# Attention and a soft mixture of experts on one core: the last term of a sum added in PSUM, a division moved behind the second layer, and loads of 2 MB in place of 1 MB

## The chip, the core and the metric

The kernel runs on one core of a Trainium2 chip. The metric is device time in microseconds (us) of one execution, as the median over runs. The core has TensorE (PE, matrix products), VectorE (DVE), ScalarE (ACT), GpSimd (POOL), and SyncE (SP), whose queue issues nearly all transfers; 16 DMA engines carry them between the main memory (HBM) and the on-chip memory (SBUF). TensorE writes its results to PSUM, from where VectorE or ScalarE copies them out. All data is 32-bit floating point.

## The reference

For 8 batches of 8 heads, with x of 512 tokens and state of 32 rows, each of width 64:

```python
# attention, per batch and head
a  = softmax(x @ state.T / 8);  xread = a  @ state     # 512 x 64
a2 = softmax(state @ x.T / 8);  sread = a2 @ x         # 32 x 64
X  = concat([xread, sread])     # all heads: 8 * 544 = 4352 tokens of width 512
# soft mixture of experts, 8 experts of 4 slots each
logits = X @ phi                                  # 4352 x 32
d = exp(logits - logits.max(0)); d /= d.sum(0) + 1e-9
slot_input = (d.T @ X).reshape(8, 4, 512)
for e in range(8):
    slot_out[e] = maximum(slot_input[e] @ w1[e], 0) @ w2[e]     # 512 -> 1024 -> 512
c = softmax(logits, axis=1)
out = c @ slot_out
```

w1 and w2 have 16.8 MB each, x 8.4 MB, the output 8.9 MB.

## The kernel before

There are three stages. The first goes through the 8 batches. A batch of x (1 MB) is turned by TensorE (`X`), scored against the state (`S`), brought to rows by VectorE's 32x32 transposes (`q`), and both softmaxes run over VectorE, GpSimd and ScalarE; `R` computes sread and is the last reader of the batch's x. Logits are computed from the attention weights without forming xread (`Lx`, with G = state times phi in `G_sb`).

The sum d.T @ X is kept as a running sum. `y` is a 128x128 tile that holds the sum so far, relative to a running maximum; each new group of two batches (0 to 3) has its exponentials `dx`, a product `T` into the PSUM tile tp, a transpose `tt`, a product `Px` with the state, and `Y`, which multiplies y by the rescaling factor `al` and adds the new term on VectorE. `Ls` to `Ys` do the same for the state's tokens. `l_row` is the running sum of the exponentials. The last steps are `Wd` (sum of l over the partitions, a product), `We` (add 1e-9 and take the reciprocal, on VectorE), `Yf` (the identity times 1/l, on ScalarE), `Y.3`, `SI` (y turned and divided in one product with that tile) and `SIe`, four copies on VectorE into two tiles si_m, from which layer 1 takes its weights. Two products `W` on a constant tile stand between them.

The order of all these steps is a list written out by hand, `ORDER`; each engine does its part in the order in which the steps are called.

The second stage is layer 1 (`w1_part`, two halves of 512 columns, 8 experts each) and the first half of layer 2's columns (`wide_part`). The third computes the rest of layer 2 in pieces (`more`) between the outputs. `so_sum` sums partial results with a product and copies them to so_r on ScalarE; `out` multiplies so_r by the softmax c, copies 2 times 2 tiles to SBUF on ScalarE and VectorE, and issues a store of 1 MB.

Loads come through pools of buffers: `big` has 13 buffers of 1 MB and `pairs` 4 of 2 MB. x takes 8 of the big ones. `todo` lists the weights in the order of loading; `load_w(n)` issues the next n, and is called at the start (13), after each batch's `R`, and inside layer 1. Issuing a load into a used buffer waits, on SP's queue, for that buffer's last readers, and for the transfer eight places before it. Five pieces of w2 go to places that other data leave (`load_part`). The last four loads (layer 3 in `todo`) are 2 MB each already.

Of the kernel before, what the change touches and what calls it, by code (L numbers as in the profile page):

```python
# [24 lines left out]
NBIG = 13  # L25
NPAIR = 4
# [27 lines left out]
Lus.1 A.7.0 lkp.1 A.6.0 dx.3 D.1 dT.3 ad.7.1 Px.2 ad.6.0 ae.7.0 dTe.3 Ps.1 al.3 Y.2 Ys.1 Lu.3 T.3 tt.3 Wd We Px.3  # L54
W.256 Yf Y.3 SI W.128 SIe
# [8 lines left out]
def attention_soft_moe(ctx: ExitStack, tc: tile.TileContext, x0, x1, x, st0, st1, w1, w2a, w2b, out_x, out_s):  # L64
# [37 lines left out]
    todo = [(1, hf, e) for hf in range(2) for e in range(E)]  # L102
    todo += [(2, k, e) for k in range(2) for e in range(0, E, 2)]
    last = todo.pop()
    todo += [(3, 0, 0), (3, 0, 4), last, (3, 1, 0), (3, 1, 4)]
    both = []

    def load_w(n):
        for _ in range(min(n, len(todo))):
            layer, k, e = todo.pop(0)  # L110
            if layer == 3:
                t = pairs.tile([P, 4 * F], F32, tag="pair", name=f"w3_{k}_{e}")
# [4 lines left out]
                continue  # L117
            if layer == 1 and len(w1t) < 8 * NPAIR:
                if not both:
                    t = pairs.tile([P, 4 * F], F32, tag="pair", name=f"w1_{k}_{e}")  # L120
                    both.extend((t[:, 0 : 2 * F], t[:, 2 * F :]))
                t = both.pop(0)
            else:
                t = big.tile([P, 2 * F], F32, tag="big", name=f"w{layer}_{k}_{e}")
            if layer == 1:
                t = t.rearrange("p (k f) -> p k f", k=4)
                nc.sync.dma_start(t, w1[k, e])
                for i in range(4):
                    w1t[k, e, i] = t[:, i]
            else:  # L130
                t = t.rearrange("p (e k f) -> p e k f", e=2, k=4)
                nc.sync.dma_start(t, w2a[e // 2, k])
                for i in range(8):
                    w2t[layer, k, e + i // 4, i % 4] = t[:, i // 4, i % 4]
# [39 lines left out]
    with ExitStack() as actx:  # L174
# [162 lines left out]
        def R_(b, h):  # L337
# [12 lines left out]
            if h == 1:  # L350
# [280 lines left out]
        def We():  # L631
            Z["rl"] = sm.tile([P, 1], F32, tag="rl", name="rl", bufs=1)
# [23 lines left out]

        def windows():
            for k in range(2):
# [3 lines left out]
        def SIe():  # L662
            for k in range(4):
                dve.tensor_copy(slots(si_m[k // 2], k % 2), Z["p"][:, k, :].rearrange("p (e c) -> p e c", c=4))
# [13 lines left out]
        (k1, e1), (k2, e2) = [todo.pop(B)[1:] for _ in range(2)]  # L678
# [16 lines left out]
        def w1_part(hf, e):  # L695
# [85 lines left out]
        def so_sum(k, half_of=0):  # L781
# [6 lines left out]
            act.copy(so_r[i // 2][:, P * (i % 2) : P * (i % 2) + P], p)  # L788

        def out(k, q):  # L790
# [12 lines left out]
            ot = big.tile([P, NJ, 512], F32, tag="big", name=f"out{k}_{q}")  # L803
# [146 lines left out]
```

## Time and profile before

| | |
|---|---|
| time, median of 3 runs | 129.68 us (129.62 to 129.85) |
| the profiled execution | 129.54 us, span 127.8 us |
| TensorE busy | 116.7 us (91%), granted clock 0.974 of full on the mean |
| VectorE, ScalarE, GpSimd busy | 86.7, 76.9, 44.8 us |
| bytes moved by DMA | 51.74 MB, mean 405 GB/s |
| layer 1 starts | 76.01 us |
| first output issued, last output issued | 102.17 us, 121.24 us |

The span runs from the first to the last instruction; the rest of an execution's time lies around it. Busy shares are over the whole span, and a kernel like this one has stages with different limits: to judge a change, the stretch in which it acts has to be read. A load that is issued early lands late without any harm, as long as the queue in front of it is full; what counts is the rate at which the queue is worked off.

### The profile page before, as it was taken

What the parts mean: (1) busy time and instruction counts of PE and PEld (TensorE: products, weight loads), DVE (VectorE), ACT (ScalarE), POOL (GpSimd) and SP (SyncE); (2) the same over time, 40 slices, a digit from 0 to 9 for tenths busy, and PEclk for the clock granted to TensorE, in tenths of its full rate; (3) what the DMA queues carried; (4) which work ended last, traced back from release to release, by engine and by line L of the source; (5) the groups of instructions that cost most, each with busy time, mean ns of one, the idle gap of its engine ahead of it and who ended that gap; (6) DMA issues with size and microseconds to landing.
All of it is one profiled execution on the core that took longest, in us unless ns stands there. A gap on an engine that the chain in (4) does not pass through costs nothing.

```text
span 127.8 us, 4698 instructions
## 1 busy us (share of the span) xinstructions
PE 116.7 (91%) x1992; PEld 80.5 (63%) x1992; DVE 86.7 (68%) x194; ACT 76.9 (60%) x189; POOL 44.8 (35%) x63
## 2 busy tenths in 40 slices
PE   5989999999999999999999999999999999998600
PEld 2737686789686869858767869952465655575200
DVE  2348999999999999999986759019930355442700
ACT  4039999999999999999965711310100445635700
POOL 3005266391947467557882105803500000000000
PEclk9999999999999999999999999999999999999955
DMA  4999999999999999999999999999999999999993
GB/s 130 345 410 423 423 426 423 428 423 421 423 423 426 416 436 416 421 431 418 426 418 433 416 421 398 448 423 441 413 441 415 436 383 412 421 419 420 386 430 139
DMA packets 8229, 51.74 MB, mean 405 GB/s; under 512 B 912, under 2 KB 1040, under 8 KB 3216
## 3 DMA queue, kind: packets, MB, share of 16 engines
q1 hardware_dynamic: 7920, 50.92, 95.9%
q10 hardware_dynamic: 288, 0.52, 1.1%
q8 instruction: 15, 0.25, 0.7%
q14 instruction: 6, 0.05, 0.1%
HBM read 42.53 MB, written 8.91 MB: 403 GB/s over the span
## 4 chain that ended last, share of the span: by engine, by line
PE 72%; DVE 10%; DMA 6%; ACT 3%; issue 2%; SPq 1%; POOL 0%; DVEq 0%; ACTq 0%; POOLq 0%
PE so_ps L760 12%; PE h_ps L697 11%; PE xt_ps L226 8%; PE o L796 7%; DMA st_phi<-st_in 6%; PE sc L245 5%; PE sr_ps L343 4%; PE an_ps L309 4%; PE eT_ps L309 4%; PE lt L378 3%; PE t_ps L503 2%; DVE sums L274 2%; DVE q L258 2%; DVE aT L290 1%; DVE m L263 1%
## 5 line engine op out<-in xcount | busy, mean ns | idle before, releaser
L267 POOL TENSOR_TENSOR q<-q,m 128x512 f32<-128x512 f32 x16 | 16.8, 1051 | 15.7 <-DVE m L263 5.2
L231 ACT ACTIVATE xt<-xt_ps 128x512 f32<-128x512 f32 x30 | 18.0, 618 | 5.7 <-PE xt_ps L226 5.5
L226 PE MATMUL xt_ps<-ident,x 128*128 128x128 f32 x128 | 18.4, 282 | 0.5 <-DMA x<-x_in 0.5
L285 POOL TENSOR_TENSOR q<-q,rr 128x512 f32<-128x512 f32 x16 | 16.6, 1051 | 5.1 <-DVE rr L280 3.6
L226 PEld LDWEIGHTS xt_ps<-ident,x 128*128 128x128 f32 x128 | 14.6, 144 | 3.8 <-PE sc L245 1.4
L760 PE MATMUL so_ps<-w,h_m 128*32 128x128 f32 (+1 forms) x376 | 15.5, 309 | 0.0
L807 DVE COPY out<-o 128x512 f32<-128x512 f32 x14 | 9.2, 687 | 9.0 <-PE o L796 8.8
L760 PEld LDWEIGHTS so_ps<-w,h_m 128*32 128x32 f32 x376 | 10.4, 110 | 7.2 <-issue 4.6
L697 PE MATMUL h_ps<-w,si_m 128*32 128x512 f32 x128 | 14.4, 594 | 0.1
L296 DVE TENSOR_REDUCE nm<-sc 128x1 f32<-128x512 f32 x16 | 10.6, 670 | 2.2 <-PE sc L245 2.2
L806 ACT COPY out<-o 128x512 f32<-128x512 f32 x14 | 7.7, 588 | 6.8 <-PE o L796 6.7
L697 PEld LDWEIGHTS h_ps<-w,si_m 128*32 128x32 f32 x128 | 9.1, 110 | 3.9 <-issue 2.9
L301 ACT ACTIVATE e<-sc,nm 128x512 f32<-128x512 f32 x16 | 11.3, 709 | 0.4 <-DVE nm L296 0.2
L258 DVE STREAM_TRANSPOSE q<-sc 128x512 f32<-128x512 f32 x16 | 11.1, 695 | 0.1
L290 DVE STREAM_TRANSPOSE aT<-q 128x512 f32<-128x512 f32 x16 | 10.9, 689 | 0.3 <-POOL q L285 0.2
L343 PE MATMUL sr_ps<-x,eT 128*32 128x64 f32 x512 | 10.5, 221 | 0.1
L274 DVE TENSOR_REDUCE sums<-q 128x16 f32<-128x512 f32 x16 | 10.4, 663 | 0.2 <-ACT q L270 0.2
L263 DVE TENSOR_REDUCE m<-q 128x16 f32<-128x512 f32 x16 | 10.4, 658 | 0.0
L270 ACT ACTIVATE q<-q 128x512 f32<-128x512 f32 x16 | 10.4, 650 | 0.0
L309 PE MATMUL eT_ps<-ident,e 128*128 128x128 f32 x64 | 9.8, 279 | 0.0
L245 PE MATMUL sc<-xt,st_phi 64*32 64x512 f32 x128 | 9.6, 601 | 0.0
L343 PEld LDWEIGHTS sr_ps<-x,eT 128*32 128x32 f32 x512 | 8.7, 110 | 1.5 <-issue 1.0
(126 smaller groups left out, 186.2 us busy)
## 6 DMA issues: line engine op xcount, KB each, us to landing
w<-w_in SPq DMA_DIRECT2D x16, 1024.0 KB, 19.7
w<-w2b_in SPq DMA_DIRECT2D x4, 2048.0 KB, 15.0
x<-x_in SPq DMA_DIRECT2D x7, 1024.0 KB, 13.9
w<-w2a_in SPq DMA_DIRECT2D x6, 1024.0 KB, 19.5
out_x<-out SPq DMA_DIRECT2D x6, 1024.0 KB, 5.8
out_x<-out SPq DMA_DIRECT2D x4, 512.0 KB, 4.7
w<-w2a_in SPq DMA_DIRECT2D x4, 256.0 KB, 14.5
x<-x_in ACTq DMA_DIRECT2D x2, 256.0 KB, 3.9
```

The lines of the kernel that those rows point to most:

```text
L226: pe.transpose(p[:, P * j : P * j + P], xb[b][:, g, j, :], ident)
L231: act.mul(r[f"xt{g}"], r[f"xp{g}"], 0.125)
L245: pe.matmul(r[f"sp{h}"][32 * g : 32 * g + 32, :], st_t(b, g)[64 * h : 64 * h + 64, :], r[f"xt{g}"][64 * h : 64 * h + 64, :], start=True, s ...
L258: dve.transpose(r[f"q{h}"], r[f"sp{h}"])
L267: pool.tensor_tensor(v, v, R[b][f"m1{h}"].broadcast_to([P, 16, NS]), op=ALU.subtract)
L274: dve.tensor_reduce(out=v, in_=R[b][f"qv{h}"], axis=AX.X, op=ALU.add)
L285: pool.tensor_tensor(v, v, r.broadcast_to([P, 16, NS]), op=ALU.mult)
L290: dve.transpose(r[f"aT{h}"], r[f"q{h}"])
L309: pe.transpose(p[:, j, :], r[f"{src}{h}"][:, P * j : P * j + P], ident)
L343: pe.matmul(r["srp"][32 * g : 32 * g + 32, h, :], r[f"eT{h}"][:, j, 32 * g : 32 * g + 32], xb[b][:, g, j, D * h : D * h + D], start=(j == ...
L697: pe.matmul(h_ps[hf][32 * kt : 32 * kt + 32, :], si_m[kt // 2][:, 256 * (kt % 2) + 32 * e : 256 * (kt % 2) + 32 * e + 32], w1t[hf, e, kt], ...
L760: pe.matmul(so[k][32 * i : 32 * i + 32, :], h_m[hf][:, 256 * i + 32 * e : 256 * i + 32 * e + 32], w(i), start=(hf == 0 and e == 0), stop=( ...
```

## The change

Loads: `big` has 3 buffers and `pairs` 9, all of x lies in pairs, and x4 with x5, x6 with x7, six pairs of experts of w1, and two quarters of w2 (`w2c`, a new input array made of the same numbers) come in one transfer of 2 MB each. Two pairs of w1 still come in two transfers. The order of the weights changes: three loads of w2 now stand before the last three pairs of w1. `load_w` is called after four batches instead of all. Outputs take halves of pairs. No byte is added.

The sum: `Px.3` and `Y.3` are gone. `SIa` turns y and multiplies it by the last factor al (the identity times al, `Yf`), leaving the sum open in PSUM; `ttz` transposes tp in two halves of 64 rows into a cleared tile tz (the place of `G_sb`, cleared by GpSimd in `windows`); `SIb` adds the state times tz into the same PSUM tiles. The copies `SIe` alternate between VectorE and ScalarE. 1/l is no longer part of it; `so_sum` multiplies by it, which is the same since maximum(., 0) passes a positive factor. The two `W` products are gone.

```diff
-NBIG = 13
-NPAIR = 4
+NBIG = 3
+NPAIR = 9
...
-Lus.1 A.7.0 lkp.1 A.6.0 dx.3 D.1 dT.3 ad.7.1 Px.2 ad.6.0 ae.7.0 dTe.3 Ps.1 al.3 Y.2 Ys.1 Lu.3 T.3 tt.3 Wd We Px.3
-W.256 Yf Y.3 SI W.128 SIe
+Lus.1 A.7.0 lkp.1 A.6.0 dx.3 D.1 dT.3 ad.7.1 Px.2 ad.6.0 ae.7.0 dTe.3 Ps.1 al.3 Y.2 Yf Ys.1 Lu.3 T.3 ttz SIa Wd We SIb
+SIe
...
-        t = big.tile([P, 4, NJ, 2 * D], F32, tag="big", name=f"x{b}")
+        if b % 2 == 0:
+            two = pairs.tile([P, 2, 4, NJ, 2 * D], F32, tag="pair", name=f"x{b}")
+        t = two[:, b % 2]
...
-        else:
-            nc.sync.dma_start(t, x[b - 2].rearrange("p (g j c) -> p g j c", g=4, j=NJ))
+        elif b < 4:
+            nc.sync.dma_start(t, x2[b - 2].rearrange("p (g j c) -> p g j c", g=4, j=NJ))
+        elif b % 2:
+            nc.sync.dma_start(two, x[b // 2 - 2].rearrange("p (b g j c) -> p b g j c", b=2, g=4, j=NJ))
...
-    todo = [(1, hf, e) for hf in range(2) for e in range(E)]
-    todo += [(2, k, e) for k in range(2) for e in range(0, E, 2)]
-    last = todo.pop()
-    todo += [(3, 0, 0), (3, 0, 4), last, (3, 1, 0), (3, 1, 4)]
-    both = []
+    todo = [(1, hf, e) for hf in range(2) for e in range(0, E, 2)]
+    todo[5:5] = [(2, 0, 0), (2, 0, 2), (2, 0, 4)]
+    todo += [(4, 0, 0), (3, 0, 0), (3, 0, 4), (2, 1, 6), (3, 1, 0), (3, 1, 4)]
...
+            elif layer == 1:
+                t = t.rearrange("p (e k f) -> p e k f", e=2, k=4)
+                if (k, e) in ((0, 2), (1, 4)):
+                    for i in range(2):
+                        nc.sync.dma_start(t[:, i], w1[k, e // 2, :, i])
+                else:
+                    nc.sync.dma_start(t, w1[k, e // 2])
+                for i in range(8):
+                    w1t[k, e + i // 4, i % 4] = t[:, i // 4, i % 4]
+            elif layer == 4:
+                t = t.rearrange("p (n e k f) -> p n e k f", n=2, e=2, k=4)
+                nc.sync.dma_start(t, w2c)
...
-            if h == 1:
+            if (b, h) in ((1, 1), (3, 1), (5, 1), (6, 1)):
                 load_w(1)
...
         def Yf():
             Z["rd"] = sm.tile([P, P], F32, tag="ds", name="rd", bufs=1)
-            act.mul(Z["rd"], ident, Z["rl"])
-
-        def SI():
-            Z["p"] = mtile([P, 4, NS], "si_ps")
-            pe.matmul(Z["p"].rearrange("p k n -> p (k n)"), y, Z["rd"], start=True, stop=True)
+            act.mul(Z["rd"], ident, al_all[:, X2[-1]["c"]])
+
+        def ttz():
+            for gh in range(2):
+                rows = slice(64 * gh, 64 * gh + 64)
+                dve.transpose(
+                    tz[rows, gh].rearrange("p g h n -> p (g h n)"),
+                    X2[-1]["tp"][rows].rearrange("p g h n -> p (g h n)"),
+                )
+
+        def SIa():
+            Z["p"] = [mtile([P, 2, NS], f"si_ps{g2}") for g2 in range(2)]
+            rd = Z["rd"].rearrange("p (a g n) -> p a g n", a=2, g=2)
+            for g2 in range(2):
+                for h in range(2):
+                    pe.matmul(
+                        Z["p"][g2][64 * h : 64 * h + 64],
+                        y[:, D * h : D * h + D],
+                        rd[:, :, g2, :],
+                        start=True,
+                        stop=False,
+                    )
+
+        def SIb():
+            for g2 in range(2):
+                for h in range(2):
+                    pe.matmul(
+                        Z["p"][g2][64 * h : 64 * h + 64],
+                        Q[1]["st"][:, 2 + g2, D * h : D * h + D],
+                        tz[:, :, g2, h, :],
+                        start=False,
+                        stop=True,
+                    )
...
         def windows():
+            pool.memset(tz, 0.0)
...
             for k in range(4):
-                dve.tensor_copy(slots(si_m[k // 2], k % 2), Z["p"][:, k, :].rearrange("p (e c) -> p e c", c=4))
+                v = Z["p"][k % 2][:, k // 2, :].rearrange("p (e c) -> p e c", c=4)
+                copy_of(act if k % 2 else dve)(slots(si_m[k // 2], k % 2), v)
...
-            if (hf, e) in ((0, 1), (0, 3)):
+            if (hf, e) in ((0, 1), (0, 3), (1, 1)):
                 load_w(1)
             if (hf, e) == (1, 0):
-                load_w(3)
+                load_w(2)
...
-            act.copy(so_r[i // 2][:, P * (i % 2) : P * (i % 2) + P], p)
+            act.mul(so_r[i // 2][:, P * (i % 2) : P * (i % 2) + P], p, Z["rl"])
...
-            ot = big.tile([P, NJ, 512], F32, tag="big", name=f"out{k}_{q}")
+            if not homes_of_out:
+                t = pairs.tile([P, 2, NJ, 512], F32, tag="pair", name=f"out{k}_{q}")
+                homes_of_out.extend((t[:, 0], t[:, 1]))
+            ot = homes_of_out.pop(0)
```

The first place is TensorE between the last product T (t_ps) and layer 1 (h_ps). A row is one instruction with its line, output, inputs and size, and the semaphores of the engines that it waits for. l_ps is `Wd`, px_ps `Px.3`, si_ps the slot inputs. Before:

```order
L503 MATMUL t_ps_1608<-an_1583,dT_1596 32x128
L629 MATMUL l_ps<-l_row,rep 128x1 [waits DVE_49,Pool_49]
L540 MATMUL px_ps_1632<-sv,tt_1625 32x64 [waits DVE_49]
L540 MATMUL px_ps_1632<-sv,tt_1625 32x64 x7
L646 MATMUL warm_ps<-ident 128x256
L642 MATMUL si_ps<-rd,y 128x128 [waits DVE_49,Activation_49]
L646 MATMUL warm_ps<-ident 128x128
L697 MATMUL h_ps_1656<-w_0_0_129,si_m_1315 32x512 [waits DMAHW5_49,DVE_49]
```

And now:

```order
L510 MATMUL t_ps_1593<-an_1566,dT_1579 32x128
L660 MATMUL si_ps_1612<-rd,y 64x64 [waits DVE_49,Activation_49]
L660 MATMUL si_ps_1612<-rd,y 64x64
L660 MATMUL si_ps_1613<-rd,y 64x64 [waits PE_49]
L660 MATMUL si_ps_1613<-rd,y 64x64
L636 MATMUL l_ps<-l_row,rep 128x1 [waits DVE_49,PE_49,Pool_49]
L671 MATMUL si_ps_1612<-G_sb,sv 64x64 x2
L671 MATMUL si_ps_1613<-G_sb,sv 64x64 x2
L736 MATMUL h_ps_1633<-w_0_0_123,si_m_1298 32x512 [waits DMAHW3_49,DVE_49]
L736 MATMUL h_ps_1633<-w_0_0_123,si_m_1298 32x512 [waits Activation_49]
```

The product for l moved behind the first si products. The pool of PSUM tiles gives it the place that t_ps had, so it waits for VectorE's transposes of t_ps, and the closing si products, which need these transposes too, have no wait of their own behind it.

The second place is VectorE in the same stretch. Before:

```order
L455 SCALAR_TENSOR_TENSOR y<-y,al_all,ps_ps_1598 128x128 [waits DVE_49,PE_49,Activation_49]
L514 STREAM_TRANSPOSE tt_1625<-t_ps_1608 128x128 [waits PE_49]
L633 TENSOR_SCALAR rl<-l_ps 128x1 [waits PE_49]
L634 RECIPROCAL rl<-rl 128x1 [waits DVE_49]
L455 SCALAR_TENSOR_TENSOR y<-y,al_all,px_ps_1632 128x128 [waits PE_49,Activation_49]
L664 COPY si_m_1315<-si_ps 128x8x4 [waits PE_49]
```

And now:

```order
L462 SCALAR_TENSOR_TENSOR y<-y,al_all,ps_ps_1581 128x128 [waits DVE_49,PE_49,Activation_49]
L650 STREAM_TRANSPOSE G_sb<-t_ps_1593 64x128 [waits PE_49]
L650 STREAM_TRANSPOSE G_sb<-t_ps_1593 64x128
L640 TENSOR_SCALAR rl<-l_ps 128x1 [waits PE_49]
L641 RECIPROCAL rl<-rl 128x1 [waits DVE_49]
L703 COPY si_m_1298<-si_ps_1612 128x8x4 [waits PE_49]
L703 COPY si_m_1300<-si_ps_1612 128x8x4
```

One update of y is gone, the transpose is in two, and the two operations on rl stay ahead of the copies.

The third place is SP's queue, where the weights of layer 1 and the first of layer 2 are issued. Before:

```order
L127 DMA w_1_3_147<-w_in 128x2048 [waits DMAHW0_49]
L127 DMA w_1_4_149<-w_in 128x2048 [waits DMAHW1_49]
L127 DMA w_1_5_368<-w_in 128x2048 [waits DMAHW2_49,PE_49]
L127 DMA w_1_6_502<-w_in 128x2048 [waits DMAHW3_49,PE_49]
L127 DMA w_1_7_645<-w_in 128x2048 [waits DMAHW4_49,PE_49]
L132 DMA w_0_0_810<-w2a_in 128x2048 [waits DMAHW5_49,PE_49]
```

And now:

```order
L128 DMA w_1_0_132<-w_in 128x4096 [waits DMAHW0_49]
L139 DMA w_0_0_134<-w2a_in 128x2048 [waits DMAHW1_49]
L139 DMA w_0_2_136<-w2a_in 128x2048 [waits DMAHW2_49]
L139 DMA w_0_4_138<-w2a_in 128x2048 [waits DMAHW3_49]
L128 DMA w_1_2_489<-w_in 128x4096 [waits DMAHW4_49,PE_49]
L126 DMA w_1_4_795<-w_in 128x2048 [waits DMAHW5_49,PE_49]
L126 DMA w_1_4_795<-w_in 128x2048 [waits DMAHW6_49]
L128 DMA w_1_6_1106<-w_in 128x4096 [waits DMAHW7_49,PE_49]
L133 DMA w_0_0_1387<-w2c_in 128x4096 [waits DMAHW0_49,PE_49]
```

The last number is elements per partition (2048 are 1 MB, 4096 are 2 MB). Each load still waits for the one eight places before it, and from w_1_2 on for TensorE's reads of the batches whose buffer it takes.

## Rows read from the trace of the kernel before

**Rows 1.** The page: DMA share in 40 slices, packets, and the queue of instruction loads.

```profile
DMA  4999999999999999999999999999999999999993
...
DMA packets 8229, 51.74 MB, mean 405 GB/s; under 512 B 912, under 2 KB 1040, under 8 KB 3216
...
q8 instruction: 15, 0.25, 0.7%
```

**Rows 2.** Stretches near the end: columns end in PEclk, DMA share, GB/s.

```profile
119.00:119.50 0.50, 0.50 (x6) 0.21 (x4) 0.23 (x1) 0.30 (x1) 0.00 (x0) 1.00 0.56 238
...
125.00:126.00 1.00, 0.00 (x0) 0.00 (x0) 0.00 (x0) 0.00 (x0) 0.00 (x0) 0.50 0.51 213
```

**Rows 3.** Timeline of SP's queue: start and length in us, DMAs issued.

```profile
78.24 2.04 SPq L114 DMA_DIRECT2D w<-w2b_in  x2
...
118.67 0.97 SPq L834 DMA_DIRECT2D out_x<-out  x2
...
121.24 0.35 SPq L811 DMA_DIRECT2D out_x<-out  x1
```

**Rows 4.** DMAs issued from 118.6 to 119.2 us: KB, us to landing.

```profile
out_x<-out SPq DMA_DIRECT2D x1, 512.0 KB, 3.8
```

**Rows 5.** DMAs issued from 121 to 122 us: KB, us to landing.

```profile
out_x<-out SPq DMA_DIRECT2D x1, 1024.0 KB, 5.6
```

**Rows 6.** DMA traffic from 20 to 70 us, and the w2a loads issued there.

```profile
DMA packets 2898, 21.19 MB, mean 424 GB/s; under 512 B 320, under 2 KB 320, under 8 KB 320
...
w<-w2a_in SPq DMA_DIRECT2D x5, 1024.0 KB, 20.7
```

**Rows 7.** DMA traffic from 86 to 100 us.

```profile
DMA packets 484, 5.99 MB, mean 428 GB/s; under 512 B 54, under 2 KB 54, under 8 KB 54
```

**Rows 8.** The stretch from 85 to 101 us, columns as in rows 2.

```profile
85.00:101.00 16.00, 15.78 (x213) 7.68 (x212) 7.90 (x23) 1.39 (x4) 2.71 (x3) 1.00 1.01 429
```

**Rows 9.** Loads of x2 to x7 (L93): issue times, and us to landing.

```profile
L93 SPq DMA_DIRECT2D x<-x_in x6: 328/424/584, 3.1 to 6.3; - x6
...
DMA to landing us min/median/max: 9.3/14.6/19.7
```

**Rows 10.** Timeline of TensorE from 23.6 us: the first transposes of x4.

```profile
24.34 0.60 PE L226 MATMUL xt_ps<-ident,x 128*128 128x128 f32 x4
```

**Rows 11.** Timeline of VectorE from 73 us.

```profile
73.81 0.32 DVE L514 STREAM_TRANSPOSE tt<-t_ps 128x128 f32<-128x128 f32 x1 [0.41 <-PE t_ps L503]
...
74.25 0.16 DVE L634 RECIPROCAL rl<-rl 128x1 f32<-128x1 f32 x1
...
75.77 0.48 DVE L664 COPY si_m<-si_ps 128x32 f32<-128x32 f32 x4 [0.64 <-PE si_ps L642]
```

**Rows 12.** Timeline of TensorE from 72.6 us.

```profile
73.64 0.38 PE L629 MATMUL l_ps<-l_row,rep 128*128 128x1 f32 x2
74.18 0.45 PE L540 MATMUL px_ps<-sv,tt 64*32 64x64 f32 x16 [0.15 <-DVE tt L514]
...
76.01 0.71 PE L697 MATMUL h_ps<-w,si_m 128*32 128x512 f32 x2
```

**Rows 13.** The copies so_r (L788): ns min/median/max, and who waited, us.

```profile
L788 ACT COPY so_r<-sum_ps x4: 266/266/284, 99.5 to 116.7; 128x128 f32<-128x128 f32 x4
...
  PEld o L823: 0.5, 1
...
  PEld os L841: 0.2, 1
```

**Rows 14.** Timeline of ScalarE: the multiplication by a column.

```profile
74.45 0.40 ACT L638 ACTIVATE rd<-ident,rl 128x128 f32<-128x128 f32 x1 [1.74 <-DVE rl L634]
```

**Rows 15.** Timeline of GpSimd from 58 us.

```profile
58.67 0.99 POOL L660 MEMSET si_m<- 128x512 f32 x2
59.62 2.20 POOL L267 TENSOR_TENSOR q<-q,m 128x512 f32<-128x512 f32 x2
```

**Rows 16.** Timeline of ScalarE from 61.9 us.

```profile
62.04 0.63 ACT L270 ACTIVATE q<-q 128x512 f32<-128x512 f32 x1
```

More of the change, by code (lines that the diff above doesn't have):

```diff
@@ L110, in load_w @@
             layer, k, e = todo.pop(0)
+            if layer == 2 and k == 0:
+                t = big.tile([P, 2 * F], F32, tag="big", name=f"w2_{k}_{e}")
+            else:
+                t = pairs.tile([P, 4 * F], F32, tag="pair", name=f"w{layer}_{k}_{e}")
             if layer == 3:
-                t = pairs.tile([P, 4 * F], F32, tag="pair", name=f"w3_{k}_{e}")
                 t = t.rearrange("p (e k f) -> p e k f", e=4, k=8)
@@ L116, in load_w @@
                     w2t[3, k, e + i // 8, i % 8] = t[:, i // 8, i % 8]
[L117 to L122, printed above, removed]
-            else:
[L124 to L131, printed above, removed]
+            elif layer == 1:
[3 more added lines that the diff above has]
+                        nc.sync.dma_start(t[:, i], w1[k, e // 2, :, i])
+                else:
+                    nc.sync.dma_start(t, w1[k, e // 2])
[4 more added lines that the diff above has]
+                nc.sync.dma_start(t, w2c)
+                for i in range(8):
+                    w2t[2, 0, 6 + i // 4, i % 4] = t[:, 0, i // 4, i % 4]
+                    w2t[2, 1, i // 4, i % 4] = t[:, 1, i // 4, i % 4]
+            else:
+                t = t[:, 0 : 2 * F].rearrange("p (e k f) -> p e k f", e=2, k=4)
                 nc.sync.dma_start(t, w2a[e // 2, k])
                 for i in range(8):
-                    w2t[layer, k, e + i // 4, i % 4] = t[:, i // 4, i % 4]
+                    w2t[2, k, e + i // 4, i % 4] = t[:, i // 4, i % 4]
     def load_part(t, k, e, ft):
@@ L631, in We @@
         def We():
-            Z["rl"] = sm.tile([P, 1], F32, tag="rl", name="rl", bufs=1)
+            Z["rl"] = cp.tile([P, 1], F32, name="rl")
             dve.tensor_scalar_add(Z["rl"], Z["lp"], EPS)
@@ L655, in attention_soft_moe @@
         si_m = []
+        tz = G_sb[:, 0:4].rearrange("p b g n -> p (b g n)").rearrange("p (a g h n) -> p a g h n", a=2, g=2, h=2)
         def windows():
+            pool.memset(tz, 0.0)
             for k in range(2):
@@ L677, in attention_soft_moe @@
         halves_had = max(order.index(t) for t in order if t.split(".")[0] in ("q", "aT", "e2", "ee", "ed", "windows"))
-        (k1, e1), (k2, e2) = [todo.pop(B)[1:] for _ in range(2)]
+        (k1, e1), (k2, e2) = (1, 2), (1, 4)
         for i, step in enumerate(order):
@@ L787, in so_sum @@
                 so_r[i // 2] = half(f"so_r{i // 2}")[:, 0:256]
-            act.copy(so_r[i // 2][:, P * (i % 2) : P * (i % 2) + P], p)
+            act.mul(so_r[i // 2][:, P * (i % 2) : P * (i % 2) + P], p, Z["rl"])
+        homes_of_out = []
         def out(k, q):
@@ L816, in out_by_batches @@
             o = [h.tile([P, 256], F32, tag=tag, name=f"o{k}_{q}_{i}") for i, (h, tag) in enumerate(homes)]
-            ot = big.tile([P, 2, NJ, 256], F32, tag="big", name=f"out{k}_{q}")
+            ot = big.tile([P, 2 * F], F32, tag="big", name=f"out{k}_{q}").rearrange("p (i j s) -> p i j s", i=2, j=NJ)
             to = out_x[k, q].rearrange("p j s -> (p j s)").rearrange("(i p j s) -> i p j s", i=2, p=P, j=NJ)
@@ L928 @@
         "x1_in": con(xl[1]),
-        "x_in": con(xl[2:]),
+        "x2_in": con(xl[2:4]),
+        "x_in": con(xl[4:].reshape(2, 2, P, -1).transpose(0, 2, 1, 3)).reshape(2, P, -1),
         "st0_in": con(sl[:, 0:1]),
@@ L932 @@
             [sl[:, 1:4].reshape(P, -1), moe_phi.reshape(4, 2, D, NS).transpose(1, 2, 0, 3).reshape(P, 4 * NS)], axis=1)),
-        "w1_in": con(moe_w1.reshape(E, 4, P, 2, 512).transpose(3, 0, 2, 1, 4)),
-        "w2a_in": con(moe_w2[:, :, :256].reshape(E // 2, 2, 2, 4, P, 256).transpose(0, 2, 4, 1, 3, 5)),
+        "w1_in": con(moe_w1.reshape(E // 2, 2, 4, P, 2, 512).transpose(4, 0, 3, 1, 2, 5)),
+        "w2a_in": (wa := con(moe_w2[:, :, :256].reshape(E // 2, 2, 2, 4, P, 256).transpose(0, 2, 4, 1, 3, 5))),
+        "w2c_in": con(_np.stack([wa[3, 0], wa[0, 1]], axis=1)),
         "w2b_in": con(moe_w2[:, :, 256:].reshape(E // 4, 4, 8, P, 2, P).transpose(0, 4, 3, 1, 2, 5)),
```

6 lines of the change are left out of this document (3 added, 3 removed).

## Prediction

> **What bounds the kernel now.** I read the page first: TensorE is busy nearly all the span, which would make it the suspect, but the DMA row of the 40 slices is full from the second slice to the last but one, and 51.74 MB pass in 127.8 us [rows 1]. So two things run side by side through the whole kernel, one chain of compute and one stream of bytes, and the question is which of them sets the end. The tail answers it. Between 119.0 and 119.5 us the share of the 16 DMA engines falls to 0.56, and at the end it is 0.51 between 125 and 126 us [rows 2]. Had the engines been emptied together, the share would have gone to nothing in the first gap, and the end would be sharp. It reads as some half of the engines that run dry for a moment while the others, which are behind, go on. The last transfer says the same: 0.5 MB issued at 118.67 us landed 3.8 us later, and 1 MB issued at 121.24 us landed 5.6 us later [rows 3 to 5]. At 424 GB/s [rows 6] the first needs 1.24 us for its bytes, so at most 2.56 us are latency; the second, with 2.47 us of bytes and that latency, would have landed after 5.03 us on empty engines. It waited at least 0.57 us behind others. So the engines that end last have a backlog at the very end, and the compute chain, which issues its last transfer at 121.24 us, has at least that much room. I take it that the end is set by the stream: start, bytes by rate, landing.
>
> **The loads.** No byte is added or removed. Eighteen loads of 1 MB become nine of 2 MB: x4 with x5, x6 with x7, six pairs of the first layer, and one mixed load of the second layer. What a 2 MB load is worth the trace shows, since four of them are there already. Between 20 and 70 us, where the queue works off loads of 1 MB, 21.19 MB pass in 50 us, or 2.360 us for a MB; between 86 and 100 us, nearly all loads of 2 MB with rows of 16 KB, 5.99 MB pass in 14 us, 2.337 us for a MB [rows 6, 7]. In both stretches the engines are never short of work. The nine loads carry 18.87 MB (nine times 2.097), times 0.0226 is 0.42 us. Bounds: nothing, if the difference between the stretches has another cause than the size (fewer instruction loads between them, say), and 18.87 x (1/0.424 - 1/0.429) = 0.52 us with the rate of 85 to 101 us [rows 8]. I take 0.42, because its stretch holds the cleanest run of 2 MB loads. All nine come before the last loads of the second layer, so these, and the outputs behind them, can start that much earlier.
>
> [...]
>
> Does a later issue cost anything? A buffer of 2 MB is free only when both halves are read, so x0's place waits for x1's readers, and so on. Loads are issued some 20.7 us before they land [rows 6], since eight of them are in flight, and now these are up to 2 MB each; a release that comes one batch later goes out in good time. The first load of the third kind, issued at 78.24 us [rows 3], waits for the first pieces of layer 1; these come earlier by the gain below (0.60 us) and the loads before it end 0.42 us earlier, so its cover grows. x4 now lands with x5. The six loads that now change were issued until 6.3 us and the last landed 19.7 us later, at 26.0 us [rows 9]; two loads (2 x 2.47 us) before that, at 21.1 us, x5 was there. TensorE takes x4 first at 24.34 us [rows 10]: 3.2 us of cover, nothing on the path. x6 and x7 are read much later.
>
> **The chain to layer 1.** Before: from the transpose of the last tp at 73.81 us [rows 11] to the first product of layer 1 at 76.01 us [rows 12] it takes 2.20 us, through px, y, the scaled identity, si and the four copies. After: the two half transposes stand between 0.32 us (one after the other in no more time than the whole one) and 0.64 us (twice the row); I take 0.52, until 74.33. In the new order the product for l stands behind them and waits for them (its bank of PSUM is tp's), queued before the four closing products: 0.38 us [rows 12], until 74.76 with a hop of 0.05. The closing products (half as many as px's 16, twice as wide) I take at 0.40, near px's 0.45 [rows 12], until 75.1. On VectorE the two small operations for 1/l now wait for l and stand ahead of the copies: 0.16 us each [rows 11], so 74.8 to 75.17. The first copy starts there; from copy to product it was 76.01 - 75.77 = 0.24 us [rows 11, 12], so layer 1 starts at 75.41. Gain 0.60 us. With 0.64 for the transposes and 0.15 more for the products and hops it is 0.3, with 0.32 for the transposes 0.8. The two warming products go with the wait that they filled.
>
> **The division.** The four evictions so_r now multiply by 1/l. As a copy one takes 0.27 us [rows 13]; the multiplication by a column, rd, takes 0.40 us for the same shape [rows 14]. For two of the four TensorE waits (0.2 and 0.5 us of idle [rows 13]), so twice 0.13 us on the chain, 0.26 in all; bounds nothing and 0.26. The other two have work of TensorE beside them.
>
> **The clearing of G_sb** on GpSimd: two clearings of 512 columns take 0.99 us, so 256 columns about 0.25 us. The two subtractions behind it end at 61.82 us, and ScalarE takes the second at 62.04 us [rows 15, 16]: 0.22 us of the 0.25 are covered, the rest has ScalarE's own queue beside it. I count nothing; without cover it is 0.25 us.
>
> **Sum.** The compute chain gains 0.60 - 0.26 = 0.34 us at the last outputs (0.05 to 0.8). The stream gains 0.42 us (0 to 0.52). They move by nearly the same, so whoever sets the end still does: the engines that end last keep their backlog of at least 0.57 us, less 0.08 us. The end moves by 0.42 us: 129.54 us of the profiled execution become 129.12; the median of the runs shown is 0.14 us above that execution, so 129.26. I say 129.25 us.
>
> **The rivals.**
> [...]
>
> Second, the compute chain sets the end: if the gap at 119 us is what delays the engines that end last, the time follows the issue at 118.67 us, and gains 0.34 us (0.05 to 0.8): 129.34. For it: the dip of [rows 2] comes right before that transfer's bytes. Against: the 0.57 us of waiting at 121.24 us, which was measured behind just that transfer, though, and so doesn't exclude it.
>
> Third, on the slower side: instructions are loaded by the same 16 engines, 15 packets that take 0.7% of 16 engines' span [rows 1], that is 0.007 x 16 x 127.8 / 15 = 0.95 us of one engine each. At the end half of the engines idle through a whole microsecond while the others go on [rows 2], and such packets are the one thing in the trace that need not fall evenly on them. The change makes other instructions (SP loses nine DMAs, TensorE some products), so the engine that ends last may get one more of them: plus 0.95 - 0.42 = 0.53 us, 130.2. It decides as soon as one packet moves onto that engine. For it: the end hangs on the last engine alone. Against: the programs are nearly equally long, so the packets should fall as they did. Half as likely, it gets one less: 129.54 - 0.42 - 0.95 and 0.14, 128.3.
>
> **How the numbers follow.** Forecast 0.50 (of it 0.04 within 0.2%, if only 0.3 or less of the 0.42 comes). Merging buys nothing 0.21. The chain sets the end 0.14 (two thirds of it faster). One instruction load more 0.10, one less 0.05. What a measurement of this kernel can tell from no change is about 0.2%, 0.26 us. Faster by more: 0.46 + 0.09 + 0.05 = 0.60; within: 0.04 + 0.21 + 0.04 = 0.29, with 0.01 of the chain on either side rounded; slower 0.11. The range goes from 128.75 us (the chain's upper bound of 0.8 us, and 0.1 of scatter) to 129.8 us (no change with the scatter of the runs); it leaves out the two cases with an instruction load, 0.15 together. The forecast's own range is 129.1 to 129.45.
>
> **What would show it.** In the profile after: 2 MB loads before 70 us with a rate near 428 GB/s; layer 1 starting near 75.4 us (a start after 75.8 makes that part wrong); so_r at 0.40 us; the last load's bytes ending some 0.4 us earlier; the last output issued near 120.9 us and still waiting over 0.4 us behind others. The forecast is wrong if the rate before 70 us stays at 424, if the last 1 MB lands within 5.1 us of its issue (then the chain set the end), or if the stretch of half-idle engines at the end grows or shrinks by about 1 us.

## The result, and the profile after

The changed kernel takes 130.64 us (median of 9 runs), the kernel before 129.94 us beside it: a ratio of 1.0063, with a 95% interval of 1.0040 to 1.0087. It is slower by 0.6%, where 0.3% faster was forecast. The profiled execution took 131.03 us with a span of 129.3 us.

First the page of the kernel after: span, packets, and the queues with their packets, MB and share of the 16 engines' span.

```profile
span 129.3 us, 4673 instructions
...
DMA packets 6933, 51.74 MB, mean 400 GB/s; under 512 B 768, under 2 KB 896, under 8 KB 3072
...
q1 hardware_dynamic: 6624, 50.92, 95.1%
...
q8 instruction: 15, 0.25, 0.8%
```

The bytes are the same [rows 1], there are 1296 packets fewer, as nine merged loads should give, and yet the mean rate fell from 405 to 400 GB/s. Where, the windows say (columns as in rows 2).

```profile
20.00:70.00 50.00, 49.53 (x1053) 38.00 (x1054) 47.88 (x106) 47.10 (x122) 31.26 (x40) 1.00 1.01 420
...
85.00:101.00 16.00, 15.63 (x209) 7.47 (x212) 7.89 (x23) 1.59 (x4) 2.71 (x3) 1.00 1.01 422
119.00:119.50 0.50, 0.50 (x6) 0.12 (x4) 0.50 (x2) 0.50 (x3) 0.00 (x0) 1.00 0.86 361
125.00:126.00 1.00, 0.00 (x0) 0.00 (x0) 0.00 (x0) 0.00 (x0) 0.00 (x0) 0.50 1.01 420
126.00:127.00 1.00, 0.00 (x0) 0.00 (x0) 0.00 (x0) 0.00 (x0) 0.00 (x0) 0.50 0.40 164
```

Everywhere: 420 instead of 424 GB/s between 20 and 70 us [rows 6], though of the new sum only the clearing at 59.12 us (shown below) has run by then, and 422 instead of 429 between 85 and 101 us [rows 8]. The DMA share is 1.01 in both, so the engines had work and did it more slowly. What is left over shows at the end: the gap at 119 us is nearly closed, and the engines are still full between 125 and 126 us, where half of them were idle before [rows 2].

Now the chain to layer 1, on the timelines of TensorE and, in the second fence, of VectorE, with one row of GpSimd in the third.

```profile
73.15 1.06 PE L510 MATMUL t_ps<-an,dT 128*32 128x128 f32 x32
74.14 0.68 PE L660 MATMUL si_ps<-rd,y 128*64 128x64 f32 x8
75.09 0.35 PE L636 MATMUL l_ps<-l_row,rep 128*128 128x1 f32 x2 [0.28 <-DVE G_sb L650]
75.37 0.45 PE L671 MATMUL si_ps<-G_sb,sv 128*64 128x64 f32 x8
76.00 1.59 PE L736 MATMUL h_ps<-w,si_m 128*32 128x512 f32 x11 [0.18 <-DVE si_m L703]
```

```profile
74.30 0.64 DVE L650 STREAM_TRANSPOSE G_sb<-t_ps 64x128 f32<-64x128 f32 x2 [0.41 <-PE t_ps L510]
75.48 0.16 DVE L640 TENSOR_SCALAR rl<-l_ps 128x1 f32<-128x1 f32 x1 [0.54 <-PE l_ps L636]
75.67 0.17 DVE L641 RECIPROCAL rl<-rl 128x1 f32<-128x1 f32 x1
```

```profile
59.12 0.31 POOL L695 MEMSET G_sb<- 128x256 f32 x1
```

Layer 1 starts at 76.00 us, as before [rows 12], because everything ahead of it was late: the transpose of the last tp starts at 74.30 instead of 73.81 us [rows 11]. From that transpose to layer 1 it now takes 1.70 us instead of 2.20. The lateness is as old as the second batch: TensorE's first transposes of x1, before and now.

```profile
8.98 1.50 PE L226 MATMUL xt_ps<-ident,x 128*128 128x128 f32 x12 [0.52 <-DMA x<-x_in]
```

```profile
9.53 1.50 PE L233 MATMUL xt_ps<-ident,x 128*128 128x128 f32 x12 [0.99 <-DMA x<-x_in]
```

From there to the product T it takes 63.68 us before (T starts at 72.66 us) and 63.62 now, so none of the lateness arises in between. In the profiled executions of the other kernels x1 is taken between 8.74 and 9.40 us, at whatever address its buffer lies: this half microsecond is for the most part scatter between executions.

The copies so_r, with one of those that waited for them; then the transfers issued from 118 to 119.3 and from 121 to 122.5 us (KB each, us to landing); then SP's timeline.

```profile
L827 ACT ACTIVATE so_r<-sum_ps,rl x4: 367/368/385, 99.8 to 117.0; 128x128 f32<-128x128 f32 x4
...
  PE o L867: 0.5, 1
```

```profile
out_x<-out SPq DMA_DIRECT2D x1, 512.0 KB, 5.1
...
out_x<-out SPq DMA_DIRECT2D x1, 1024.0 KB, 6.5
```

```profile
118.98 1.56 SPq L878 DMA_DIRECT2D out_x<-out  x2
...
121.93 1.10 SPq L855 DMA_DIRECT2D out_x<-out  x1
```

The last 1 MB is issued 0.69 us later than before and takes 0.9 us more [rows 3, 5]. In the chain of waits a load of weights now stands, where the chain of before has none; start, length, what:

```profile
81.56 16.15 DMA w<-w2a_in
97.72 0.04 issue
97.76 1.11 PE so_ps L799 x16
```

TensorE catches up with the last 1 MB of w2a: the stream is so late that layer 2 waits for it, if only by 0.15 us. In after_rl_back, the changed kernel with its buffers at their old address (below), the chain of waits has no load from 70 us on.

### The profile page after: what moved, and what is told of

Its sections match the earlier page's. It is cut to its first block, busy times and chain, and to the rows that moved or that the text cites. A ratio compares the mean times of both kernels' runs of the same rounds, so it can differ in the third digit from the quotient of the medians.

```text
span 129.3 us, 4673 instructions
## 1 busy us (share of the span) xinstructions
PE 116.3 (90%) x1986; PEld 78.6 (61%) x1986; DVE 86.5 (67%) x192; ACT 77.4 (60%) x191; POOL 44.9 (35%) x64
## 3 DMA queue, kind: packets, MB, share of 16 engines
q1 hardware_dynamic: 6624, 50.92, 95.1%
## 4 chain that ended last, share of the span: by engine, by line
PE 57%; DMA 19%; DVE 10%; ACT 5%; issue 2%; SPq 1%; POOL 0%; ACTq 0%; DVEq 0%; POOLq 0%
DMA w<-w2a_in 12%; PE xt_ps L233 8%; PE so_ps L799 7%; PE o L837 7%; DMA st_phi<-st_in 6%; PE sc L252 5%; PE h_ps L736 4%; PE eT_ps L316 4%; PE sr_ps L350 4%; PE an_ps L316 3%; PE lt L385 3%; PE t_ps L510 2%; DVE sums L281 2%; DVE q L265 2%; DVE m L270 1%
## 5 line engine op out<-in xcount | busy, mean ns | idle before, releaser
L736 PEld LDWEIGHTS h_ps<-w,si_m 128*32 128x32 f32 x128 | 7.3, 110 | 5.7 <-issue 2.9
L837 PE MATMUL o<-lt_all,so_r 32*128 32x512 f32 x56 | 9.4, 636 | 0.0
```

The source lines that it names most:

```text
L736: pe.matmul(h_ps[hf][32 * kt : 32 * kt + 32, :], si_m[kt // 2][:, 256 * (kt % 2) + 32 * e : 256 * (kt % 2) + 32 * e + 32], w1t[hf, e, kt], ...
L837: pe.matmul(o[j], so_r[hf][rows, col : col + 128], lt_all[rows, 4 * q : 4 * q + 4, :].rearrange("p b s -> p (b s)"), start=True, stop=True,)
```

## The experiments

Where a table or a text below speaks of engine time, it is q1's share times the span, the time that each of the 16 engines spends on the kernel's own transfers (50.92 MB in each kernel). Before it is 0.959 x 127.8 = 122.56 us; a step of the share's last digit is 0.13 us. The rates and engine times are each from one profiled execution.

| kernel | first load buffer past a multiple of 512 B | loads | sum | ratio to before (95%) | GB/s, 10 to 75 us | engine time, us |
|---|---|---|---|---|---|---|
| before | 0 | 1 MB | old | 1 | 424 | 122.56 |
| base (before again) | 0 | 1 MB | old | one run | 423 | 122.53 |
| work_shifted | 0 | 1 MB | old | 1.0003 (0.9988 to 1.0019) | 423 | 122.72 |
| sum_rl_back | 0 | 1 MB | new | 0.9992 (0.9979 to 1.0006) | 424 | 122.34 |
| loads_only | 0 | merged | old | 0.9991 (0.9970 to 1.0012) | 427 | 121.95 |
| after_rl_back | 0 | merged | new | 0.9965 (0.9951 to 0.9978) | 427 | 121.70 |
| rl_back_late | 0 | merged | new, put off 0.54 us | 0.9958 (0.9929 to 0.9988) | 427 | 122.15 |
| rl_back_later | 0 | merged | new, put off 1.40 us | 1.0044 (1.0020 to 1.0068) | 427 | 122.24 |
| after_rl256 | 256 | merged | new | 0.9965 (0.9936 to 0.9994) | 427 | 121.70 |
| after_rl128 | 128 | merged | new | 1.0020 (0.9997 to 1.0044) | 424 | 122.30 |
| after_rl64 | 64 | merged | new | 1.0036 (1.0018 to 1.0055) | 424 | 122.50 |
| after | 32 | merged | new | 1.0063 (1.0040 to 1.0087) | 423 | 122.96 |
| before_rl_moved | 32 | 1 MB | old | 1.0128 (1.0099 to 1.0156) | 417 | 123.74 |
| loads_shifted | 32 | 1 MB | old | 1.0100 (1.0074 to 1.0126) | 416 | 123.61 |
| sum_only | 32 | 1 MB | new | 1.0104 (1.0077 to 1.0132) | 417 | 123.81 |
| split | 32 | 1 MB | new | 1.0131 (1.0102 to 1.0161) | 417 | 123.73 |

Between kernels with the same loads at a multiple of 256 the engine time differs by up to 0.54 us (121.70 to 122.24 with merged loads, 122.34 to 122.72 with loads of 1 MB), so a smaller difference says nothing by itself. The rate from 10 to 75 us is steadier: 427 in all five of the former, 423 or 424 in all four of the latter.

### Which part is it?

**base** is the kernel before once more, for the scatter of its rows between executions.

> The kernel before once more, on the chip of the next three, so that traces can be compared on one chip. Every theory: 129.6 to 130.3 us; first transposes of x1 wait for their load until about 9.0 us, last load landed near 105.8 us. If x1 is as late here as in the changed kernel's profile (about 9.5 us), that half microsecond is scatter between executions and not the change.

It took 129.66 us, with 423 GB/s between 10 and 75 us and 0.51 again between 125 and 126 us, so two executions agree on the rate and the backlog. TensorE took x1 at 9.19 us, between the 8.98 us of the kernel before and the 9.53 us of the changed one.

**sum_only** is the kernel before with the sum's part of the change alone:

```diff
-... Y.2 Ys.1 Lu.3 T.3 tt.3 Wd We Px.3 W.256 Yf Y.3 SI W.128 SIe
+... Y.2 Yf Ys.1 Lu.3 T.3 ttz SIa Wd We SIb SIe
...
-            Z["rl"] = sm.tile([P, 1], F32, tag="rl", name="rl", bufs=1)
+            Z["rl"] = cp.tile([P, 1], F32, name="rl")
```

> The kernel before with the new end of the sum and the division behind the second layer, loads as before. Theory A (the stream of transfers sets the end, by the DMA engine that ends last; the 2 MB loads make that engine fall behind): ratio 0.998 to 1.002, layer 1 starts about 0.5 us earlier and the end does not move. Theory B (the new sum's waits and multiplications cost at the end): ratio 1.004 or more. Theory C (the compute chain sets the end): ratio 0.996 to 0.998.

**loads_only** is the changed kernel with the old sum, that is with these lines the other way round.

> The new loads, buffers and order of weights, with the old end of the sum. Theory A: ratio 1.004 to 1.010, like the whole change. Theory B: 0.996 to 1.000 (the merged loads gain their 0.42 us). Theory D (the order of the weights: the mixed and the late load of the second layer land late and TensorE waits for them): also 1.004 or more, with a wait of TensorE for the last 1 MB load of the second layer.

**split** is the whole change, with each new load of 2 MB issued as two of 1 MB into the halves of the same buffer (here the lines for w1; x and the mixed load of w2 are split alike):

```diff
-                if (k, e) in ((0, 2), (1, 4)):
-                    for i in range(2):
-                        nc.sync.dma_start(t[:, i], w1[k, e // 2, :, i])
-                else:
-                    nc.sync.dma_start(t, w1[k, e // 2])
+                for i in range(2):
+                    nc.sync.dma_start(t[:, i], w1[k, e + i])
```

> The whole change, but each new load of 2 MB issued as two of 1 MB from arrays laid out as before: new buffers, order and sum, old transfers. Theory A (size of the rows): ratio 0.997 to 1.001, back to the kernel before, less for the earlier chain. Theory D (order and buffers): 1.004 or more, as slow as the whole change. Theory B (sum): 1.004 or more as well.

Measured: 1.0104, 0.9991 and 1.0131. The loads are not what makes it slower; without the merging it is slower still. What makes it slower comes with the sum, though no step of the sum needs a transfer. The windows from 10 to 75 us of sum_only and of loads_only, in this order, show a loss in a stretch that lies nearly all before the sum is at work:

```profile
10.00:75.00 65.00, 63.75 (x1328) 48.89 (x1326) 60.65 (x132) 59.62 (x152) 36.71 (x48) 1.00 1.01 417
```

```profile
10.00:75.00 65.00, 64.24 (x1340) 49.39 (x1338) 61.19 (x136) 59.66 (x152) 36.51 (x47) 1.00 1.01 427
```

So the theory with which I went into this, that rows of 16 KB leave the last engine with more, fell. One line of the sum does act from the start: `rl`, a tile of 128x1, comes from the constants' pool `cp` instead of `sm`. In the built program `cp` lies ahead of all load buffers and ended at 15360, a multiple of 512; with rl's 32 bytes it ends at 15392, and every tile behind it begins 32 bytes past such a multiple.

### Is it the address?

**before_rl_moved** moves rl and nothing else; **after_rl_back** is the changed kernel with rl left where it was; **sum_rl_back** is the same for sum_only; **after_rl64** pads rl to 64 bytes.

```diff
 before_rl_moved
-            Z["rl"] = sm.tile([P, 1], F32, tag="rl", name="rl", bufs=1)
+            Z["rl"] = cp.tile([P, 1], F32, name="rl")
 after_rl_back, sum_rl_back
-            Z["rl"] = cp.tile([P, 1], F32, name="rl")
+            Z["rl"] = sm.tile([P, 1], F32, tag="rl", name="rl", bufs=1)
 after_rl64
-            Z["rl"] = cp.tile([P, 1], F32, name="rl")
+            Z["rl"] = cp.tile([P, 16], F32, name="rl")[:, 0:1]
```

> The kernel before, with nothing changed but that rl comes from the constants' pool (first load buffer at 15392); every instruction is as before. Theory E: the rate in 10 to 75 us falls from 423 to about 417 GB/s, and the ratio is 1.008 to 1.013. Rival (the new sum costs, the address does nothing): ratio 0.998 to 1.002 and rate 423.

> The changed kernel, with only the 128x1 tile rl taken from the pool sm again, as before the change, so that the SBUF address of the first load buffer is 15360 again instead of 15392 (addresses of the built program). Theory E (the 32 bytes by which rl shifts every load buffer make each load packet about 4 ns longer, and the stream sets the end): the rate in 10 to 75 us is back at 423 to 427 GB/s, q8's share at 0.7%, and the ratio to before is 0.992 to 0.999. Rival (the new sum costs by waits near the end): the rate is a matter of the sum, and the ratio stays at 1.004 to 1.009.

> The new sum and division with the loads of before, and rl back in the pool sm (first load buffer at 15360). Theory E: the rate in 10 to 75 us is 423 or more instead of 417 GB/s, and the ratio to before is 0.995 to 1.001; the sum's shorter chain (0.5 us) is worth little, since the stream sets the end. Rival (the new sum costs): ratio 1.008 to 1.013, as sum_only had.

> The changed kernel, with rl as the first column of a 128x16 tile in the constants' pool, so that the first load buffer is at 15424: 64 bytes past a multiple of 512, instead of 32. Theory E, if a multiple of 64 is all that the loads need: like the kernel with rl in its old pool, ratio 0.992 to 0.999 and rate 423 to 427. Theory E, if they need a larger multiple: ratio 1.004 to 1.009 and rate about 420. Rival (the new sum costs): 1.004 to 1.009 in both.

Measured: 1.0128, 0.9965, 0.9992 and 1.0036 (the last lies between the two ranges foretold). Theory B, that the new sum costs by its waits, fits the three ratios further above; sum_rl_back, the new sum with the old address, excludes it. The kernel before, with every instruction as it was, loses 1.3% by 32 bytes; the changed kernel gains 1% by giving them back. The pages say how: of the kernel before, of before_rl_moved, and of after_rl_back, span and q1.

```profile
span 127.8 us, 4698 instructions
...
q1 hardware_dynamic: 7920, 50.92, 95.9%
```

```profile
span 129.3 us, 4698 instructions
...
q1 hardware_dynamic: 7920, 50.92, 95.7%
```

```profile
span 127.3 us, 4673 instructions
...
q1 hardware_dynamic: 6624, 50.92, 95.6%
```

The shares hardly move, but they are shares of different spans: 122.56, 123.74 and 121.70 us. The same packets keep each engine busy 1.18 us longer. In q1's single packets, in the traces of the kernel before and of the changed one, a load's packet of 8 KB takes 313 ns in the middle instead of 309 from some 20 us on (316.1 instead of 311.0 on the mean, between 30 and 60 us), one of 16 KB 614 instead of 611 (620 instead of 615 on the mean, between 85 and 101 us). With the loads of 1 MB that would be 189 packets for each engine times 5.1 ns, and 32 times 5 ns: 1.12 us, which agrees. The packets of the outputs take 309 ns in the middle in both. A packet of 16 KB loses here about as much as one of 8 KB (5 and 5.1 ns), so merged loads should lose less by the shift than those of 1 MB; the ratios don't tell it apart (after against after_rl_back loses 0.0098, with loads of 1 MB before_rl_moved and loads_shifted against the kernel before, and sum_only against sum_rl_back, lose 0.0100 to 0.0128).

### How far must it be aligned?

**after_rl128** pads rl to 128 bytes; **after_rl256** has the four 128x1 tiles lx in the constants' pool as well, 256 bytes in all.

```diff
-            Z["rl"] = cp.tile([P, 1], F32, name="rl")
+            Z["rl"] = cp.tile([P, 32], F32, name="rl")[:, 0:1]
 after_rl256 also
-            r["lx"] = sm.tile([P, 1], F32, tag="lx", name=f"lx_{k}", bufs=4)
+            r["lx"] = cp.tile([P, 1], F32, name=f"lx_{k}")
```

> The changed kernel with rl as the first column of a 128x32 tile of the constants' pool: first load buffer at 15488, 128 bytes past a multiple of 512. With 32 bytes past it the ratio was 1.0063, with 64 bytes 1.0036, with none 0.9965. If 128 bytes are enough for the loads: 0.995 to 0.998, rate in 10 to 75 us 426 to 427 GB/s. If what counts is 256 or 512: 1.002 to 1.006, rate 420 to 424.

> The changed kernel with the first load buffer at 15616, 256 bytes past a multiple of 512 (rl as the first column of a 128x32 tile, and the four 128x1 tiles lx from the constants' pool too). If 256 bytes are enough: 0.995 to 0.998. If it takes 512: 1.001 to 1.006. If an address had nothing to do with it, and only the pool that rl is in, 1.004 to 1.009 as in the changed kernel.

Measured: 1.0020 and 0.9965. A multiple of 256 bytes is as good here as one of 512 (0.9965 in after_rl_back too), and rl's pool by itself is of no matter, since in after_rl256 it is the new one. A multiple of 128 is not enough: the ratio's interval begins just above where that of after_rl256 ends (0.9997 and 0.9994), and the rate is 424 instead of 427 GB/s. The engine time alone would not show it: 122.30 us, against 121.70 to 122.24 at a multiple of 256.

The cost does not grow from 32 to 64 to 128 bytes (ratios 1.0063, 1.0036 and 1.0020; 423, 424 and 424 GB/s from 10 to 75 us). That it falls is not shown, since neighbouring intervals overlap. Why 256 bytes are enough and 128 are not, no run shows.

### Loads or working tiles?

A shift of the constants' end moves the load buffers, and behind them the tiles on which the engines work. That the packets are still as short as before in the first 15 us (309 ns for 8 KB between 10 and 15 us, in the kernel before and in the changed one), though the buffers are off from the first load, leaves it open which of the two costs. **loads_shifted** moves the buffers by 32 bytes and fills up behind them; **work_shifted** puts rl between the two, so that only the working tiles move.

```diff
+        pad = actx.enter_context(tc.tile_pool(name="pad", bufs=1))
         wk = actx.enter_context(tc.tile_pool(name="work", bufs=1))
 loads_shifted
+        lxs = pad.tile([P, 56], F32, name="lxs")
...
-            r["lx"] = sm.tile([P, 1], F32, tag="lx", name=f"lx_{k}", bufs=4)
+            r["lx"] = lxs[:, k : k + 1]
...
-            Z["rl"] = sm.tile([P, 1], F32, tag="rl", name="rl", bufs=1)
+            Z["rl"] = cp.tile([P, 1], F32, name="rl")
 work_shifted
-            Z["rl"] = sm.tile([P, 1], F32, tag="rl", name="rl", bufs=1)
+            Z["rl"] = pad.tile([P, 1], F32, name="rl")
```

> The kernel before with rl in the constants' pool, as in before_rl_moved, so that the load and output buffers begin 32 bytes past a multiple of 512, but with a filler of 224 bytes behind them (it also holds the four 128x1 tiles lx), so that the working tiles of the engines stand at a multiple of 256 again. Theory E1 (what costs is where the loads write): ratio 1.008 to 1.014, q1's share times the span 123.6 to 123.9 us, as with everything shifted. Theory E2 (what costs is that the engines read and write working tiles at shifted addresses): 0.998 to 1.002, 122.4 to 122.7 us.

> The kernel before with rl in a pool of its own between the load buffers and the working tiles: load and output buffers at the addresses of before, working tiles 32 bytes past a multiple of 256. Theory E1 (where the loads write): ratio 0.998 to 1.002, q1's share times the span 122.4 to 122.7 us. Theory E2 (where the engines' working tiles stand): 1.008 to 1.014, 123.6 to 123.9 us.

Measured: 1.0100 and 1.0003. Moving the working tiles alone costs nothing that can be told, and moving the load buffers alone costs nearly as much as moving both. Their windows, loads_shifted first:

```profile
10.00:75.00 65.00, 63.83 (x1337) 49.02 (x1335) 60.89 (x135) 59.21 (x152) 36.46 (x47) 1.00 1.01 416
```

```profile
10.00:75.00 65.00, 64.11 (x1339) 49.30 (x1337) 60.67 (x134) 59.45 (x152) 36.46 (x47) 1.00 1.01 423
```

One stretch doesn't fit. Between 85 and 101 us, before_rl_moved and then loads_shifted:

```profile
85.00:101.00 16.00, 15.78 (x212) 7.58 (x212) 7.89 (x23) 1.38 (x4) 2.72 (x3) 1.00 1.01 422
```

```profile
85.00:101.00 16.00, 15.78 (x214) 7.66 (x212) 7.89 (x23) 1.30 (x4) 2.71 (x3) 1.00 1.01 428
```

The load buffers are off by 32 bytes in both, yet loads_shifted runs as with aligned buffers here (429 in the kernel before, [rows 8]). So the address of the load buffers is needed for the loss, but something else decides when it acts. What that is stays open; the pieces of w2 that `load_part` brings into working tiles from 75 to 84 us, just before that stretch, land at a multiple of 256 in loads_shifted and not in before_rl_moved, but whether this matters was not tried.

### Does the stream set the end?

With rl back, the compute chain is put off by one and by three warming products ahead of `SIb`.

```diff
 rl_back_late
-... T.3 ttz SIa Wd We SIb
+... T.3 ttz SIa Wd We W.256 SIb
 rl_back_later
-... T.3 ttz SIa Wd We SIb
+... T.3 ttz SIa Wd We W.256 W.256 W.256 SIb
```

> The changed kernel with rl in its old pool, and one product of ident by 256 columns (0.70 us in the trace of before) put back on TensorE ahead of the closing products, so that layer 1 starts some 0.7 us later with the same loads. If the stream of transfers sets the end, with room to spare for the compute chain: ratio unchanged, 0.995 to 0.998. If the compute chain sets it once the loads are merged: 0.70 us on top of 0.9965, 1.001 to 1.003. If the two end nearly together: in between, 0.998 to 1.001.

> As rl_back_late, with three products of ident by 256 columns instead of one, so that layer 1 starts some 1.8 to 1.9 us later than with none (one of them moved it by 0.54 us and cost less than the runs can tell: 0.9958). If the stream has room for the compute chain of 0.5 to 1 us, the end moves by the rest, 0.9 to 1.4 us: ratio 1.003 to 1.008. If the room is 2 us or more, the ratio stays at 0.996 to 0.999. If there is no room and the run before was luck: 1.010 to 1.012.

Measured: 0.9958 (0.9929 to 0.9988) and 1.0044 (1.0020 to 1.0068). The product T and layer 1 on TensorE, of after_rl_back, rl_back_late and rl_back_later:

```profile
72.93 1.06 PE L510 MATMUL t_ps<-an,dT 128*32 128x128 f32 x32
...
75.78 1.67 PE L736 MATMUL h_ps<-w,si_m 128*32 128x512 f32 x12 [0.18 <-DVE si_m L703]
```

```profile
72.63 1.06 PE L510 MATMUL t_ps<-an,dT 128*32 128x128 f32 x32
...
76.02 1.47 PE L736 MATMUL h_ps<-w,si_m 128*32 128x512 f32 x9 [0.17 <-DVE si_m L703]
```

```profile
72.34 1.06 PE L510 MATMUL t_ps<-an,dT 128*32 128x128 f32 x32
...
76.59 2.96 PE L736 MATMUL h_ps<-w,si_m 128*32 128x512 f32 x24 [0.18 <-DVE si_m L703]
```

From T to layer 1 it takes 2.85, 3.39 and 4.25 us. Put off by 0.54 us, the end doesn't move by anything that can be told; put off by 1.40 us, it moves by (1.0044 - 0.9965) x 129.7 = 1.0 us. So the compute chain has some 0.4 us of room behind the stream, between nothing and 0.9 us by the ends of the two intervals. (I had expected 1.8 us from three products; on TensorE one takes 0.68 us, and the three together 1.54.)

## Why the prediction was wrong, point by point

**The step that failed** is the list of what the change moves. It had every instruction, and of `We` it took the two operations, not the tile `rl` that they write. That line puts 32 bytes into the pool that lies ahead of all load buffers; the diff cut to its core above doesn't even show it, since I took it for nothing. The missing term is plus 1.3 us: (1.0063 - 0.9965) x 129.7 = 1.27 us of time (0.8 to 1.8 by the ends of the intervals); in engine time it is 0.7 to 1.3 us (122.96 against 121.70 to 122.24). In the prediction's own words, the failing step is "The loads. No byte is added or removed", after which each load was given the rate that [rows 6 to 8] show; that rate was one of aligned buffers.

**The end is set by the stream: right.** It is why a loss of 1 to 2% in the rate became a loss in time, and the room of some 0.4 us, rough as it is, agrees with what [rows 5] gave (at least 0.57 us, less 0.08). With aligned buffers the shorter chain alone brings nothing that can be told (sum_rl_back), as it should then.

**The merging, 0.42 us: right in sign, and in size only roughly.** The rate from 10 to 75 us rises from 423 or 424 to 427 GB/s; from 20 to 70 us it is 426 in after_rl_back, not the 428 foretold. In the engine time merging brings 0.61 us with the old sum, 0.64 with the new, 0.77 with shifted buffers, hardly more than that time's own scatter. In time, loads_only shows 0.1 us (0.4 gained to 0.2 lost), after_rl_back 0.45 us (0.3 to 0.6). That the shorter chain makes the difference is not shown: rl_back_late, which has the loads of loads_only and takes as long from T to layer 1 (3.39 and 3.35 us), gains 0.5 us (0.2 to 0.9), and all three intervals overlap.

**The chain to layer 1, 0.60 us: right in kind, 0.1 too large.** It gained 0.50. The half transposes take 0.64 us, my upper bound, not 0.52; the product for l took 0.35 us (costed at 0.38) and the closing products 0.45 (costed at 0.40). By the sign that the prediction names, a start after 75.8 us, this part would be wrong; but x1 came 0.55 us later in this execution than in that of the kernel before, and with the buffers at a multiple of 256 layer 1 starts at 75.78 (after_rl_back), 75.62 (sum_rl_back) and 75.36 us (after_rl256).

**The division, 0.40 us each: 0.37 measured** (0.27 before, [rows 13]). What it costs at the end was not measured by itself. **The clearing: 0.31 us**, 0.25 foretold; it is not in the chain of waits.

**The rivals.** The slower one was right in sign, but its mechanism is not what the runs show: there are 15 instruction loads in each kernel, and the loss is spread over the rate from some 20 us on. On which engine each of them fell, the traces don't say. That merging buys nothing is out too, since with buffers back in place it does bring something (0.9965 in after_rl_back against 0.9992 in sum_rl_back); and so is the second, since the chain could be put off by 0.54 us at no cost that can be told. The kernel as I had costed it is after_rl_back: 129.20 us measured, 129.25 foretold. It beats both kernels. That the two agree so closely is in part luck, since loads_only, where the same stream should set the same end, took 129.60 us.

**What would have shown it** was named: "if the rate before 70 us stays at 424". It fell to 420. The stretch of half-idle engines at the end neither went nor grew; it came about a microsecond later (share 0.40 between 126 and 127 us).

## What to carry to other kernels

Where a stream of loads sets the end, the address of its buffers is part of the kernel. Here 32 bytes past a multiple of 512 cost the kernel before 1.3% (1.0128, before_rl_moved), and 256 bytes past one cost nothing (0.9965 in after_rl256 and in after_rl_back). So let load buffers begin at such an address, by pools that come first or by a filler, and look at the addresses in the built program after each edit of a small tile, since the order of instructions doesn't show them. When a change slows a stretch in which none of its instructions run, look for what is fixed before the start: addresses, sizes, the place of the program. Compare transfers by engine time (share times span) rather than by share, which stayed at 95 to 96% while the time moved by 1.2 us, and look at the rate beside it, since engine time scatters by half a microsecond.

## What I had not expected of the hardware

- Where the loads' destinations in SBUF are 32 bytes off a multiple of 256 (the changed kernel against the kernel before), a load's packet of 8 KB takes 313 instead of 309 ns in the middle (1.3%) and one of 16 KB 614 instead of 611 (0.5%). With 64 and 128 bytes the rate of the merged loads from 10 to 75 us is 424 GB/s, with 32 it is 423, at a multiple of 256 it is 427: no more is lost than with 32 bytes, but not nothing.
- The shift costs nothing at first: between 10 and 15 us a packet of 8 KB takes 309 ns in the kernel before and in the changed one, and up to 20 us the latter's packets of 16 KB take 611 ns, though the destinations are off from the first load. From 85 to 101 us it costs nothing in loads_shifted (428 GB/s, 429 in the kernel before). It is not that the engines have less to do: between 10 and 15 us the DMA share is 1.04 in the changed kernel, and VectorE and ScalarE are busy for 4.01 and 4.80 of the 5 us. What switches the loss on and off is open.
- The 15 instruction loads take longer too when the buffers are off: q8's share times the span is 0.9 us in all kernels at a multiple of 256 (0.7%), and 1.0 us in the others (0.8%).
